# Decode attention and gated feed-forward on one core: products two pieces ahead of the sums, the last group's probabilities in a buffer of their own, and w_up in two loads

## The chip, the cores and the metric

The kernel runs on one core of a Trainium2 chip. The metric is the device time of one execution in microseconds (us); the time before is the median of three runs. Beside it stands one execution taken with the hardware profiler, whose span runs from its first to its last instruction.

## The reference

One token passes through an attention block with a cached K and V and then through a gated feed-forward block. All inputs are bf16.

```python
# x: [1,1,640]; K and V caches: [1,32,4096,128]; wq: [640,4096]; wo: [4096,640]
# w_gate, w_up: [640,1728]; w_down: [1728,640]
q = (layernorm(x) @ wq)                      # 32 heads of 128
p = softmax(q . K / sqrt(128))               # per head, over 4096 positions
h = x + (p . V) @ wo
h2 = h + (gelu(layernorm(h) @ w_gate) * (layernorm(h) @ w_up)) @ w_down
```

K and V of each head are read once: 32 heads x 4096 x 128 x 2 bytes is 33.6 MB for each cache.

## The kernel before

The 32 heads are worked in four groups of eight. A group's K is one load of 8.39 MB into a tile of 64 KB in each of the 128 partitions: a head takes 16 partitions, and each partition holds 256 positions of 128 values. V has the same layout. Three such tiles, `big[0]` to `big[2]`, are used in turn (`kb`, `vb`, lines 135 and 136). `wo_sb` and `wg_sb` lie in `big[2]`, after K of group 3 has been read, and `wu_sb` and `wd_sb` in `big[0]`, after V of group 2 has been read. In `big[2]`, w_o and w_gate take 58,240 of the 65,536 bytes of a partition.

The scores of a group are made in eight pieces of 32 positions per partition (`scores`, line 349). For a piece, VectorE multiplies K by the query in place (`mult`, line 323). TensorE then adds the 128 products of each position down to 16, by eight products with a unit matrix that accumulate in one PSUM bank (`fold`, line 329; its first product has line 336 and the other seven have line 285, that of the helper `again`). VectorE sums these 16 (`red`, line 341). Two PSUM banks, `pf[0]` and `pf[1]`, take turns, so a fold waits for the sum two pieces back (line 339). Each engine works its own list in the order in which the program writes it, and the order on VectorE is: product 0, product 1, sum 0, product 2, sum 1, and so on. After the fold of the second piece, `between` puts other work in: the second half of the queries, or the group before's `outs`.

`soft(g)` (line 362) takes the maximum of each head, the exponentials on ScalarE, and writes the probabilities into `P` spread over eight columns by a mask (line 374). `P` is one buffer for all groups, so this write waits for the value products of the group before (`t_pv[g - 1]`). `values(g)` (line 379) puts the sums of the exponentials into `rsm`, has TensorE add these over the partitions (line 382), and makes 64 products of P with V (line 386). `outs(g)` (line 392) divides, picks each head's own part and collects it in `aT`.

The order of the parts is written out by hand. From group 2 on it is:

```python
    scores(2, lambda: outs(1), ahead=True)   # ahead: the first product of group 3 as well
    load_v(3, kfree[2])
    soft(2)
    scores(3)
    values(2)
    soft(3)
    outs(2)
    values(3)
    t_aT = outs(3)
```

All large loads are issued from SyncE, in program order, on one queue. A load that reuses a tile waits on SyncE for the last reader: K and V loads for `kfree` (a group's last fold) or `vfree` (a group's last value product). The loads at the end are w_o and w_gate (`kfree[3]`), w_up (`vfree[2]`), and w_down in five pieces (`wd_sb`, line 440 and 445).

At the end of the program, the attention output is multiplied by w_o (line 472), normed, and multiplied by w_gate and then by w_up in `up` (line 483): five blocks of the 640 inputs, four products for each, with two short ones for the last 64 columns, for each matrix. The products with w_down follow (line 525), then the cast and the store.

Of the kernel before, what the change touches and what calls it, by code (L numbers as in the profile page):

```python
# [6 lines left out]
BF16 = mybir.dt.bfloat16  # L7
ALU = mybir.AluOpType
# [3 lines left out]
D = 640  # L12
# [3 lines left out]
DF = 1728  # L16
NC_D = D // 128
# [5 lines left out]
HG = 8  # L23
NG = H // HG
PPH = 128 // HG
R = SK // PPH
RP = 32
NP = R // RP
VR = 32 // HG
NV = R // VR  # L30
HB = 4
QD = 128 // HB
# [75 lines left out]
def bass_sequential_preLN__gqa_block_cached__glu_gated_geglu__decode_kernel(  # L108
# [12 lines left out]
    S = Sched(nc)  # L121

    def sb(name, shape, dt):
        return nc.alloc_sbuf_tensor(name, shape, dt)

    def at(name, base, off, shape, dt=BF16):
        return nc.alloc_sbuf_tensor_at(name, shape, dt, offset=nc.lookup_mloc(base).addr + off)

    big = [sb("big%d" % i, [128, R, DH], BF16) for i in range(3)]
    wq_sb = at("wq_sb", big[2], 0, [128, NC_D, H * DH])  # L130
    wo_sb = at("wo_sb", big[2], 0, [128, QD, D])
    wg_sb = at("wg_sb", big[2], 2 * QD * D, [128, NC_D, DF])
    wu_sb = at("wu_sb", big[0], 0, [128, NC_D, DF])
    wd_sb = at("wd_sb", big[0], 2 * NC_D * DF, [128, NF, D])
    kb = [big[0], big[2], big[1], big[2]]
    vb = [big[1], big[0], big[0], big[1]]
# [4 lines left out]
    qb = sb("qb", [128, NG, DH], BF16)  # L141
    sc = sb("sc", [128, R], FP32)
    ex = sb("ex", [128, R], BF16)
    P = sb("P", [128, R, HG], BF16)
    rs = sb("rs", [128, NG], FP32)
    rsm = sb("rsm", [128, HG], FP32)
    mx = sb("mx", [128, NG], FP32)
# [10 lines left out]
    hmask = sb("hmask", [128, HG], FP32)  # L158
# [26 lines left out]
    ones = sb("ones", [128, 128], FP32)  # L185
# [9 lines left out]
    pv, pg, pu = pq[0:2], pq[2], pq[3]  # L195
    pz = pm
    pd = pf[0]

    def vec(fn, waits=()):
        return S.op("vector", fn, waits)  # L200
# [20 lines left out]
    a = pick(jred, quad)  # L221
# [3 lines left out]
    t_hbf = vec(lambda v: v.tensor_copy(hmask_bf[:, :], hmask[:, :]), [t_hmask])  # L225

    kfree, vfree = [None] * NG, [None] * NG
# [39 lines left out]
    a = None  # L267
    for c in range(NC_D):
        a = S.op("tensor", lambda t, c=c: t.matmul(
            po[:, c:c + 1], x_sb[0:1, c::NC_D], ones_bf[0:1, 0:1],  # L270
            start=(c == 0), stop=(c == NC_D - 1), skip_group_check=True),
            [d_x, t_onebf], token=(c == NC_D - 1))
# [44 lines left out]
                t_qb[gg] = S.op("scalar", lambda a, gg=gg: a.copy(qb[:, gg, :], xz[:, :]), [t_qf[0]])  # L317

    fold_done, red_done = {}, {}
    t_p, t_pv, t_acc, t_rz, t_z = ([None] * NG for _ in range(5))  # L320
    t_ext, t_ex = None, None

    def mult(g, s):
        return vec(lambda v: v.tensor_tensor(  # L324
            out=kb[g][:, s * RP:(s + 1) * RP, :], in0=kb[g][:, s * RP:(s + 1) * RP, :],
            in1=qb[:, g, :].unsqueeze(1).to_broadcast([128, RP, DH]), op=ALU.mult),
            [d_k[g], t_qb[g]])

    def fold(g, s, t_mult):
        n = g * NP + s  # L330
        W = 512 // RP
        for j in range(DH // W):
            def mm(t, j=j):
                dst, src = pf[n % 2][:, :], kb[g][:, s * RP:(s + 1) * RP, j * W:(j + 1) * W]
                if j == 0:
                    return t.matmul(dst, Ibf[:, :], src, start=True, stop=False)  # L336
                return again(t, dst, Ibf[:, :], src, j == DH // W - 1)
            fold_done[n] = S.op("tensor", mm,
                [t_mult, t_ibf, red_done.get(n - 2)], token=(j == DH // W - 1))
# [7 lines left out]
    early = {}  # L347

    def scores(g, between=None, ahead=False):
        t_mul = early.pop(g, None) or mult(g, 0)  # L350
        for s in range(NP):
            fold(g, s, t_mul)
            if s + 1 < NP:
                t_mul = mult(g, s + 1)
            elif ahead:
                early[g + 1] = mult(g + 1, 0)
            if between and s == 1:
                between()
            red(g, s)
        kfree[g] = fold_done[g * NP + NP - 1]  # L360

    def soft(g):
        nonlocal t_ex
        a = vec(lambda v: v.reduce_max(mx[:, g:g + 1], sc[:, :], axis=AX.X), [red_done[g * NP + NP - 1]])
        a = vec(lambda v: v.transpose(mt[:, :], mx[:, g:g + 1].to_broadcast([128, 32])), [a])
        a = vec(lambda v: v.reduce_max(
            mh[:, :], mt[:, :].rearrange("p (t i) -> p t i", t=2), axis=AX.X), [a])
        a = vec(lambda v: v.scalar_tensor_tensor(  # L368
            out=mj[:, :], in0=mh[:, :], scalar=-SCALE, in1=tmask[:, :], op0=ALU.mult, op1=ALU.mult,
            accum_out=nb[:, g:g + 1]), [a, t_tmask])  # L370
        t_ex = S.op("scalar", lambda a: a.activation(  # L371
            ex[:, :], sc[:, :], ACTF.Exp, bias=nb[:, g:g + 1], scale=SCALE,
            accum_out=rs[:, g:g + 1]), [a, t_p[g - 1] if g else None])
        t_p[g] = vec(lambda v: v.tensor_tensor(  # L374
            out=P[:, :, :], in0=ex[:, :].unsqueeze(2).to_broadcast([128, R, HG]),
            in1=hmask_bf[:, :].unsqueeze(1).to_broadcast([128, R, HG]), op=ALU.mult),
            [t_ex, t_hbf, t_pv[g - 1] if g else None])

    def values(g):
        a = vec(lambda v: v.tensor_scalar(  # L380
            rsm[:, :], hmask[:, :], rs[:, g:g + 1], 0.0, ALU.mult, ALU.add), [t_ex, t_z[g - 1] if g else None])
        t_z[g] = S.op("tensor", lambda t: t.matmul(  # L382
            pz[:, 8:8 + HG], ones[:, :], rsm[:, :], start=True, stop=True), [a, t_rz[g - 1] if g else None])
        for i in range(NV):
            r, q = i * VR, 32 * (i % 4)
            t_pv[g] = S.op("tensor", lambda t, i=i, r=r, q=q: t.matmul(  # L386
                pv[g % 2][q:q + 32, :], P[:, r:r + VR, :], vb[g][:, r:r + VR, :],
                start=(i < 4), stop=(i >= NV - 4)),
                [t_p[g], d_v[g], t_qt[0], t_ext], token=(i == NV - 1))
        vfree[g] = t_pv[g]  # L390
# [39 lines left out]
    d_wo = S.dma("sync", "wo", lambda s: s.dma_start(  # L430
        wo_sb[:, :, :], A_wo[:, :].rearrange("(p c) n -> p c n", c=QD)), [kfree[3]])

    def load_w(name, dst, src, wait):
        return S.dma("sync", name, lambda s: s.dma_start(
            dst[:, :, :], src[:, :].rearrange("(p c) n -> p c n", c=NC_D)), [wait])

    d_wg = load_w("wg", wg_sb, B_w_gate, kfree[3])
    d_wu = load_w("wu", wu_sb, B_w_up, vfree[2])
    t_zr = S.op("gpsimd", lambda g: g.memset(wd_sb[:, NM, :], 0.0), [vfree[2]])
    d_we = S.dma("sync", "wde", lambda s: s.dma_start(  # L440
        wd_sb[E0:E0 + EP, NM, :], B_w_down[MF:DF, :]), [t_zr])
# [1 line left out]
    for i in range(len(WD_CUTS) - 1):  # L443
        lo, hi = WD_CUTS[i], WD_CUTS[i + 1]
# [6 lines left out]
    def clear(ps, t):  # L451
# [3 lines left out]
    t_clear = [clear(pg, t_qt[0]), clear(pu, t_qt[0])]  # L455

    a = vec(lambda v: v.tensor_tensor(
        out=aL[:, :, :], in0=aT[:, :].unsqueeze(2).to_broadcast([128, H, HB]),
        in1=jmask[:, :].unsqueeze(1).to_broadcast([128, H, HB]), op=ALU.mult), [t_aT, t_jm])
    a = S.op("tensor", lambda t: t.matmul(  # L460
        pz[:, 64:64 + QD], aL[:, :, :], csel[:, :], start=True, stop=True), [a, t_cs])
    t_aP = vec(lambda v: v.tensor_copy(aP[:, :], pz[:, 64:64 + QD]), [a])

    for j in range(4):
        S.op("tensor", lambda t, j=j: t.matmul(
            pd[32 * j:32 * j + 1, 0:NQ], ones_bf[0:1, 0:1], x_sb[0:1, j * NQ:(j + 1) * NQ],
            start=True, stop=False, skip_group_check=True), [red_done[NG * NP - 2]], token=False)
    b = None
    for c in range(QD):
        for j in range(4):  # L470
            last = c == QD - 1 and j == 3
            b = S.op("tensor", lambda t, c=c, j=j: t.matmul(
                pd[32 * j:32 * j + 1, 0:NQ], aP[:, c:c + 1], wo_sb[:, c, j * NQ:(j + 1) * NQ],
                start=False, stop=False, skip_group_check=True), [t_aP, d_wo], token=last)
    a = vec(lambda v: v.transpose(
        th[:, :].rearrange("p (c i) -> p c i", c=NC_D),
        pd[:, 0:NQ].rearrange("p (i c) -> p c i", c=NC_D)), [b])
    t_h = vec(lambda v: v.scalar_tensor_tensor(
        out=h32[:, :], in0=th[:, 0:NQ:32], scalar=1.0, in1=zero[:, :], op0=ALU.mult, op1=ALU.add,
        accum_out=st[:, 2:3]), [a])  # L480
    t_hln = layernorm(h32, t_h, 2, (hln[:, :], h32[:, :]), pz)

    def up(ps, w, d_w, t_clear):
        b = None
        for c in range(NC_D):
            for j in range(4):
                row = ps[32 * j:32 * j + 1, 0:32 * NF].rearrange("p (i b) -> p i b", b=NF)
                lhs = hln[:, c:c + 1]
                last = c == NC_D - 1 and j == 3
                b = S.op("tensor", lambda t, c=c, j=j, row=row, lhs=lhs: t.matmul(  # L490
                    row[:, :, 0:NM], lhs,
                    w[:, c, QF * j:QF * (j + 1)].rearrange("p (i b) -> p i b", b=NM),
                    start=(c == 0), stop=(c == NC_D - 1), skip_group_check=True),
                    [t_hln, d_w, t_clear], token=last)
                if E0 <= 32 * j < E0 + EP:
                    f0 = MF + 32 * j - E0
                    S.op("tensor", lambda t, c=c, j=j, f0=f0, row=row, lhs=lhs: again(
                        t, row[:, :, NM:NF], lhs, w[:, c, f0:f0 + 32].unsqueeze(2),
                        c == NC_D - 1, 32 * j), token=False)
        return b  # L500
# [9 lines left out]
    a = vec(lambda v: v.tensor_mul(t1[:, :], g_t, g_t), [t_g])  # L510
    a = vec(lambda v: v.tensor_mul(t2[:, :], t1[:, :], g_t), [a])
# [4 lines left out]
    a = vec(lambda v: v.reciprocal(r_t[:, :], d_t[:, :]), [a])  # L516
# [47 lines left out]
```

## Time and profile before

| | |
|---|---|
| median of three runs | 205.74 us (204.15, 205.74, 206.18) |
| the profiled execution's own time | 202.97 us |
| its span | 201.7 us |
| mean granted TensorE clock | 0.852 |
| busy: VectorE, TensorE products | 129.9 us (64%), 117.6 us (58%) |
| read from HBM | 84.23 MB, 418 GB/s over the span |

A row of the timeline has the start, the duration, the engine, the line and the operation with its tiles. In brackets stands how long the engine was idle just before it and what ended that. PE is TensorE, PEld its weight load, DVE is VectorE, ACT is ScalarE, SPq is the queue of SyncE. In the part on transfers the last figure is the time from the issue to the landing. A row for a stretch (two times with a colon) has the busy time of each engine, then the granted clock, the share of the transfer engines and GB/s.

### The profile page before, as it was taken

To read this page: it belongs to the slowest core of one execution; us is meant where nothing else is said; L and a number is where in the kernel's file an instruction comes from. 1 tells how busy PE (TensorE), PEld (TensorE's weight loads), DVE (VectorE), ACT (ScalarE), POOL (GpSimd) and SP (SyncE) were. 2 spreads that over 40 slices of the span, in tenths; PEclk is the share of its full clock that TensorE was granted. 3 is DMA by queue.
4 is the path that set the end of the run, shared out by engine and by line. 5 is a ranking of instruction groups with operands and counts; after the bars stand their busy time and mean duration, and the time that the engine had idled before them with its cause. 6 is when DMAs were issued, how large, how long until landed. Compare 5 with 4: busy or idle time off the path is not lost.

```text
span 201.7 us, 1610 instructions
## 1 busy us (share of the span) xinstructions
PE 117.6 (58%) x826; PEld 22.0 (11%) x552; DVE 129.9 (64%) x162; ACT 6.0 (3%) x18; POOL 1.1 (1%) x6
## 2 busy tenths in 40 slices
PE   1008383591686199497627464776197777194554
PEld 1001000000000041100003100000000003143312
DVE  5100530889898737899962598999889973804231
ACT  3000000001000100000010000000100001000000
POOL 0000000000000000000000000000000000100000
PEclk9999969679589958859985999999958999969855
DMA  7999999999999999999999999999999999999992
GB/s 260 406 556 429 429 416 416 416 416 416 416 416 482 494 455 406 429 429 416 429 416 416 419 455 507 429 429 429 416 429 416 429 416 448 393 420 417 425 401 82
DMA packets 2400, 84.32 MB, mean 418 GB/s; under 512 B 281, under 2 KB 474, under 8 KB 858
## 3 DMA queue, kind: packets, MB, share of 16 engines
q1 hardware_dynamic: 2392, 84.23, 97.1%
q8 instruction: 5, 0.08, 0.2%
q10 hardware_dynamic: 2, 0.00, 0.0%
q14 instruction: 1, 0.01, 0.0%
HBM read 84.23 MB, written 0.00 MB: 418 GB/s over the span
## 4 chain that ended last, share of the span: by engine, by line
DMA 46%; DVE 36%; PE 15%; issue 1%; ACT 1%; SPq 0%; DVEq 0%
DMA big<-in_A_k_cache_dram 34%; DVE big L324 23%; DMA wu_sb<-in_B_w_up_dram 11%; PE pf L285 6%; DVE sc L343 6%; PE pq L386 5%; DVE P L374 2%; PE pf L336 1%; DVE xm L309 1%; PE pq L490 1%; PE pf L525 1%; DVE xz L314 1%; ACT ex L371 1%; DVE xz L398 1%; PE pm L382 0%
## 5 line engine op out<-in xcount | busy, mean ns | idle before, releaser
L324 DVE TENSOR_TENSOR big<-big,qb 128x4096 bf16<-128x4096 bf16 x32 | 72.8, 2282 | 17.8 <-DMA big<-in_A_k_cache_dram 17.8
L285 PE MATMUL pf<-big,Ibf 128*128 128x512 bf16 x224 | 63.0, 428 | 0.0
L336 PE MATMUL pf<-big,Ibf 128*128 128x512 bf16 x32 | 14.3, 446 | 34.2 <-DVE big L324 34.2
L343 DVE TENSOR_REDUCE sc<-pf 128x32 f32<-128x512 f32 x32 | 21.9, 686 | 9.1 <-PE pf L285 9.0
L386 PE MATMUL pq<-big,P 128*32 128x512 bf16 x256 | 20.6, 494 | 0.0
L309 DVE TENSOR_TENSOR xm<-pq,hmask 64x512 f32<-64x512 f32 x8 | 5.5, 688 | 16.1 <-PE pq L285 15.9
L299 PE MATMUL pq<-wq_sb,xb 128*128 128x512 bf16 x10 | 4.8, 475 | 15.6 <-DMA wq_sb<-in_A_wq_dram 11.6
L336 PEld LDWEIGHTS pf<-big,Ibf 128*128 128x128 bf16 x32 | 3.5, 111 | 94.5 <-DVE big L324 94.1
L374 DVE TENSOR_TENSOR P<-ex,hmask_bf 128x2048 bf16<-128x2048 bf16 x4 | 9.2, 2292 | 5.1 <-PE pq L386 3.1
L285 PE MATMUL pq<-wq_sb,xb 128*128 128x512 bf16 x30 | 10.7, 476 | 0.0
L386 PEld LDWEIGHTS pq<-big,P 128*32 128x32 bf16 x256 | 7.8, 121 | 10.9 <-issue 7.8
L382 PE MATMUL pm<-rsm,ones 128*128 128x8 f32 x8 | 2.2, 345 | 11.3 <-DVE rsm L380 11.3
L401 PE MATMUL po<-hsel,xz 128*128 128x8 f32 x8 | 1.8, 293 | 11.7 <-DVE xz L398 11.7
L395 DVE TENSOR_TENSOR xm<-pq,rmask 128x512 f32<-128x512 f32 x4 | 2.6, 652 | 4.8 <-PE pq L386 4.8
L371 ACT ACTIVATE ex<-sc,nb 128x256 bf16<-128x256 f32 x4 | 2.0, 507 | 117.2 <-DVE mj L368 117.2
L314 DVE TENSOR_REDUCE xz<-xm 128x128 f32<-128x512 f32 x4 | 4.1, 1022 | 0.1
L398 DVE TENSOR_REDUCE xz<-xm 128x128 f32<-128x512 f32 x4 | 4.1, 1018 | 0.1
L299 PEld LDWEIGHTS pq<-wq_sb,xb 128*128 128x128 bf16 x10 | 1.2, 120 | 25.6 <-issue 20.4
L382 PEld LDWEIGHTS pm<-rsm,ones 128*128 128x128 f32 x8 | 1.8, 280 | 16.8 <-DVE rsm L380 16.8
L490 PE MATMUL pq<-wu_sb,hln 128*1 128x416 bf16 x20 | 2.2, 566 | 1.9 <-DMA wu_sb<-in_B_w_up_dram 1.9
L401 PEld LDWEIGHTS po<-hsel,xz 128*128 128x128 f32 x8 | 1.4, 218 | 16.5 <-DVE xz L398 16.5
L490 PE MATMUL pq<-wg_sb,hln 128*1 128x416 bf16 x20 | 2.2, 562 | 1.2 <-DVE hln L264 1.2
(76 smaller groups left out, 37.6 us busy)
## 6 DMA issues: line engine op xcount, KB each, us to landing
wq_sb<-in_A_wq_dram SPq DMA_DIRECT2D x1, 5120.0 KB, 15.1
wo_sb<-in_A_wo_dram SPq DMA_DIRECT2D x1, 5120.0 KB, 17.4
wg_sb<-in_B_w_gate_dram SPq DMA_DIRECT2D x1, 2160.0 KB, 22.2
wu_sb<-in_B_w_up_dram SPq DMA_DIRECT2D x1, 2160.0 KB, 22.8
wd_sb<-in_B_w_down_dram SPq DMA_DIRECT2D x1, 800.0 KB, 23.5
wd_sb<-in_B_w_down_dram SPq DMA_DIRECT2D x1, 640.0 KB, 23.7
wd_sb<-in_B_w_down_dram SPq DMA_DIRECT2D x1, 480.0 KB, 24.4
wd_sb<-in_B_w_down_dram SPq DMA_DIRECT2D x1, 160.0 KB, 24.3
```

What stands on the lines that cost most here:

```text
L285: return t.add_instruction(m)
L299: return t.matmul(dst, xb[:, c, :], src, start=(c == 0), stop=last)
L309: a = t_qt[0] = vec(lambda v, i=i, lo=lo, hi=hi, h0=h0: v.tensor_tensor(out=xm[lo:hi, :, :], in0=pq[i][lo:hi, :].rearrange("p (h d) -> p h ...
L314: t_qf[0] = vec(lambda v: v.reduce_sum(xz[:, :], xm[:, :, :].rearrange("p h d -> p d h"), axis=AX.X), [a, t_qb[gg - 1] if gg else None])
L324: return vec(lambda v: v.tensor_tensor(out=kb[g][:, s * RP:(s + 1) * RP, :], in0=kb[g][:, s * RP:(s + 1) * RP, :], in1=qb[:, g, :].unsquee ...
L336: return t.matmul(dst, Ibf[:, :], src, start=True, stop=False)
L343: red_done[n] = vec(lambda v: v.reduce_sum(sc[:, s * RP:(s + 1) * RP], pf[n % 2][:, :].rearrange("p (r w) -> p r w", r=RP), axis=AX.X), [f ...
L371: t_ex = S.op("scalar", lambda a: a.activation(ex[:, :], sc[:, :], ACTF.Exp, bias=nb[:, g:g + 1], scale=SCALE, accum_out=rs[:, g:g + 1]), ...
L374: t_p[g] = vec(lambda v: v.tensor_tensor(out=P[:, :, :], in0=ex[:, :].unsqueeze(2).to_broadcast([128, R, HG]), in1=hmask_bf[:, :].unsqueez ...
L386: t_pv[g] = S.op("tensor", lambda t, i=i, r=r, q=q: t.matmul(pv[g % 2][q:q + 32, :], P[:, r:r + VR, :], vb[g][:, r:r + VR, :], start=(i < ...
L398: t_ext = vec(lambda v: v.reduce_sum(xz[:, :], xm[:, :, :].rearrange("p r d -> p d r"), axis=AX.X), [a, t_acc[g - 1] if g else t_qb[NG - 1]])
L490: b = S.op("tensor", lambda t, c=c, j=j, row=row, lhs=lhs: t.matmul(row[:, :, 0:NM], lhs, w[:, c, QF * j:QF * (j + 1)].rearrange("p (i b) ...
```

## The change

Three things change. First, `scores` keeps two products ahead of the sums instead of one (`LOOK = 2`): VectorE's order becomes product 0, 1, 2, sum 0, product 3, sum 1, and so on, with the last three sums of a group in a row. With `ahead`, the first two products of group 3 stand among the last sums of group 2. Second, the probabilities of group 3 go to `Pl`, a buffer of 4 KB in each partition behind w_gate in `big[2]`; their write waits for the last fold of group 3 (`kfree[3]`), no longer for the value products of group 2. `rsm` is now written in `soft`, right behind the probabilities, and no longer in `values`. Third, w_up is loaded in two parts, three fifths and two fifths of its blocks, and each block's products wait for their own part. The lines below `LOOK` move down by one to three.

```diff
+LOOK = 2
...
-    P = sb("P", [128, R, HG], BF16)
+    P = [sb("P", [128, R, HG], BF16)] * (NG - 1) + [at("Pl", big[2], 2 * (QD * D + NC_D * DF), [128, R, HG])]
...
     def scores(g, between=None, ahead=False):
-        t_mul = early.pop(g, None) or mult(g, 0)
+        t_mul = early.pop(g, None) or {s: mult(g, s) for s in range(LOOK)}
+        nxt = early.setdefault(g + 1, {}) if ahead else {}
         for s in range(NP):
-            fold(g, s, t_mul)
-            if s + 1 < NP:
-                t_mul = mult(g, s + 1)
+            fold(g, s, t_mul[s])
+            if s + LOOK < NP:
+                t_mul[s + LOOK] = mult(g, s + LOOK)
             elif ahead:
-                early[g + 1] = mult(g + 1, 0)
+                nxt[s + LOOK - NP] = mult(g + 1, s + LOOK - NP)
             if between and s == 1:
                 between()
             red(g, s)
...
         t_p[g] = vec(lambda v: v.tensor_tensor(
-            out=P[:, :, :], in0=ex[:, :].unsqueeze(2).to_broadcast([128, R, HG]),
+            out=P[g][:, :, :], in0=ex[:, :].unsqueeze(2).to_broadcast([128, R, HG]),
             in1=hmask_bf[:, :].unsqueeze(1).to_broadcast([128, R, HG]), op=ALU.mult),
-            [t_ex, t_hbf, t_pv[g - 1] if g else None])
+            [t_ex, t_hbf, kfree[g] if g == NG - 1 else t_pv[g - 1] if g else None])
+        t_rs[g] = vec(lambda v: v.tensor_scalar(
+            rsm[:, :], hmask[:, :], rs[:, g:g + 1], 0.0, ALU.mult, ALU.add), [t_ex, t_z[g - 1] if g else None])
 
     def values(g):
-        a = vec(lambda v: v.tensor_scalar(
-            rsm[:, :], hmask[:, :], rs[:, g:g + 1], 0.0, ALU.mult, ALU.add), [t_ex, t_z[g - 1] if g else None])
         t_z[g] = S.op("tensor", lambda t: t.matmul(
-            pz[:, 8:8 + HG], ones[:, :], rsm[:, :], start=True, stop=True), [a, t_rz[g - 1] if g else None])
+            pz[:, 8:8 + HG], ones[:, :], rsm[:, :], start=True, stop=True), [t_rs[g], t_rz[g - 1] if g else None])
...
-    def load_w(name, dst, src, wait):
-        return S.dma("sync", name, lambda s: s.dma_start(
-            dst[:, :, :], src[:, :].rearrange("(p c) n -> p c n", c=NC_D)), [wait])
-
-    d_wg = load_w("wg", wg_sb, B_w_gate, kfree[3])
-    d_wu = load_w("wu", wu_sb, B_w_up, vfree[2])
+    def load_w(name, dst, src, lo, hi, wait):
+        return [S.dma("sync", name, lambda s: s.dma_start(
+            dst[:, lo:hi, :], src[:, :].rearrange("(p c) n -> p c n", c=NC_D)[:, lo:hi, :]), [wait])] * (hi - lo)
+
+    d_wg = load_w("wg", wg_sb, B_w_gate, 0, NC_D, kfree[3])
+    d_wu = load_w("wu", wu_sb, B_w_up, 0, 3, vfree[2])
+    d_wu += load_w("wv", wu_sb, B_w_up, 3, NC_D, vfree[2])
...
-                    [t_hln, d_w, t_clear], token=last)
+                    [t_hln, d_w[c], t_clear], token=last)
```

More of the change, by code (lines that the diff above doesn't have):

```diff
@@ L319, in bass_sequential_preLN__gqa_block_cached__glu_gated_geglu__decode_kernel @@
     fold_done, red_done = {}, {}
-    t_p, t_pv, t_acc, t_rz, t_z = ([None] * NG for _ in range(5))
+    t_p, t_pv, t_acc, t_rz, t_rs, t_z = ([None] * NG for _ in range(6))
     t_ext, t_ex = None, None
@@ L386, in values @@
             t_pv[g] = S.op("tensor", lambda t, i=i, r=r, q=q: t.matmul(
-                pv[g % 2][q:q + 32, :], P[:, r:r + VR, :], vb[g][:, r:r + VR, :],
+                pv[g % 2][q:q + 32, :], P[g][:, r:r + VR, :], vb[g][:, r:r + VR, :],
                 start=(i < 4), stop=(i >= NV - 4)),
```

## The prediction

> **What bounds the kernel now.** First the page: the DMA row in slices, the bytes, and the chain that ended last.
>
> ```profile
> DMA  7999999999999999999999999999999999999992
> HBM read 84.23 MB, written 0.00 MB: 418 GB/s over the span
> DMA 46%; DVE 36%; PE 15%; issue 1%; ACT 1%; SPq 0%; DVEq 0%
> ```
>
> The chain gives VectorE 36%, which invites work on VectorE. The first row corrects that: the transfers are busy in every slice but the first and the last, also where the chain runs over VectorE. The chain in order of time shows their pace.
>
> ```profile
> 1.25 33.99 DMA big<-in_A_k_cache_dram
> ...
> 78.07 35.22 DMA big<-in_A_k_cache_dram
> ```
>
> K of group 0 lands at 1.25 + 33.99 = 35.24, K of group 2 at 113.29. Between them land V0, K1, V1 and K2, four loads of 8.39 MB (128 x 64 KB): 78.05 / 4 = 19.5 us each, 430 GB/s. K3, V2 and V3 follow, so V3 lands near 113.29 + 3 x 19.5 = 171.8. 84.23 MB at 430 GB/s are 196 us of a span of 201.7: the transfer stream has some 3 us of room besides its start and the output.
>
> Next, what is issued last, when it lands (page, last part), and the timeline of the end.
>
> ```profile
> wq_sb<-in_A_wq_dram SPq DMA_DIRECT2D x1, 5120.0 KB, 15.1
> wo_sb<-in_A_wo_dram SPq DMA_DIRECT2D x1, 5120.0 KB, 17.4
> wg_sb<-in_B_w_gate_dram SPq DMA_DIRECT2D x1, 2160.0 KB, 22.2
> wu_sb<-in_B_w_up_dram SPq DMA_DIRECT2D x1, 2160.0 KB, 22.8
> wd_sb<-in_B_w_down_dram SPq DMA_DIRECT2D x1, 800.0 KB, 23.5
> wd_sb<-in_B_w_down_dram SPq DMA_DIRECT2D x1, 640.0 KB, 23.7
> wd_sb<-in_B_w_down_dram SPq DMA_DIRECT2D x1, 480.0 KB, 24.4
> wd_sb<-in_B_w_down_dram SPq DMA_DIRECT2D x1, 160.0 KB, 24.3
> wd_sb<-in_B_w_down_dram SPq DMA_DIRECT2D x1, 80.0 KB, 22.3
> ```
>
> ```profile
> 166.43 0.33 SPq L430 DMA_DIRECT2D wo_sb<-in_A_wo_dram  x1
> 166.80 0.43 SPq L434 DMA_DIRECT2D wg_sb<-in_B_w_gate_dram  x1
> ...
> 194.16 0.91 PE L490 MATMUL pq<-wu_sb,hln 128*1 128x416 bf16 x5 [1.92 <-DMA wu_sb<-in_B_w_up_dram]
> ...
> 197.51 2.15 PE L525 MATMUL pf<-wd_sb,hm 128*1 128x160 bf16 x56 [1.04 <-DVE hm L519]
> 198.95 0.23 PEld L525 LDWEIGHTS pf<-wd_sb,hm 128*1 128x1 bf16 x12 [0.28 <-DMA wd_sb<-in_B_w_down_dram]
> 199.34 0.09 PEld L525 LDWEIGHTS pf<-wd_sb,hm 128*1 128x1 bf16 x4 [0.16 <-DMA wd_sb<-in_B_w_down_dram]
> ```
>
> w_o lands at 166.43 + 17.4 = 183.8, w_gate at 166.80 + 22.2 = 189.0, w_up at 194.1, where its wait ends. The last products wait for two pieces of w_down, at 198.95 and 199.34. So in this execution the end is the landing of the last piece of w_down plus four products, the cast and the store. The arithmetic runs ahead of the loads by little: w_up's products were held 1.92 us by their load, and the last products lost 0.28 + 0.16. Arithmetic may thus be 1.92 + 0.44 = 2.4 us later before it sets the end. The stream has a second margin: w_o must be issued before V3 is through. Its issue needs at most 2.9 us to take effect (wq: 15.1 us for 5.24 MB that take 12.2 at 430 GB/s), so 166.43 + 2.9 = 169.3 against 171.8, 2.5 us. Both margins are about 2.4 us.
>
> **The change part by part.** Its span lies around group 3, in this timeline.
>
> ```profile
> 146.71 0.61 PE L336 MATMUL pf<-big,Ibf 128*128 128x512 bf16 x1 [4.99 <-DVE big L324]
> 147.11 3.19 PE L285 MATMUL pf<-big,Ibf 128*128 128x512 bf16 x7
> 150.34 0.69 DVE L343 TENSOR_REDUCE sc<-pf 128x32 f32<-128x512 f32 x1 [0.89 <-PE pf L285]
> ...
> 164.72 1.67 PE L285 MATMUL pf<-big,Ibf 128*128 128x512 bf16 x7
> 166.43 0.69 DVE L343 TENSOR_REDUCE sc<-pf 128x32 f32<-128x512 f32 x1 [1.40 <-PE pf L285]
> ...
> 167.64 3.64 PE L386 MATMUL pq<-big,P 128*32 128x512 bf16 x64
> ...
> 168.70 0.19 ACT L371 ACTIVATION_READ_ACCUMULATOR ex<-sc,nb 128x1 f32 x1
> ...
> 171.40 2.29 DVE L374 TENSOR_TENSOR P<-ex,hmask_bf 128x2048 bf16<-128x2048 bf16 x1 [3.14 <-PE pq L386]
> ...
> 176.78 5.05 PE L386 MATMUL pq<-big,P 128*32 128x512 bf16 x64
> ...
> 185.13 2.38 PE L472 MATMUL pf<-wo_sb,aP 128*1 128x160 bf16 x128
> 189.94 0.91 PE L490 MATMUL pq<-wg_sb,hln 128*1 128x416 bf16 x5 [1.18 <-DVE hln L264]
> ```
>
> *Products two ahead.* The same 32 products and 32 sums are issued, in another order; nothing is added. A fold still needs the sum two pieces back, since there are two PSUM banks (line 339). Before, the eighth product of a group follows sum 5; after, it precedes it, but its fold must wait for sum 5. Either way the last fold of a group starts after 8 products and 6 sums. At full clock the edit gives nothing. What it does take away are sums that wait for a slow fold in mid-group: here 0.89 us at 150.34. All such waits are in one row:
>
> ```profile
> DVE sc L343 <- PE pf L285: 9.0, 8, 1.5
> ```
>
> Four of the eight are the group ends, as the 1.40 at 166.43, and stay. Those of groups 0 and 1 can only bring forward the issue of K and V loads, and the DMA row shows the queue never empty there. On group 3 I take 0.9 (bounds 0 and 0.9): last fold and w_o's issue at 165.5 instead of 166.4. The price of its cover: products held in front of the first sum delay nothing, as no transfer waits for a sum.
>
> *rsm moved into the softmax, probabilities of group 3 in Pl.* One operation changes place, none is added. Before, group 2's value products began at 167.64, behind the last sum and rsm, 1.25 after the last fold; after, they need only their own small sum product: 165.5 + 0.4 = 165.9, done at 169.6. So w_up is issued 1.7 us earlier, behind w_gate in the queue either way: nothing. P of group 3 waited on VectorE, idle for 3.14 us, until those products were done at 171.3; behind it stood rz, xm, xz and aT of group 2. In its own buffer it needs the exponentials (168.9) and the last fold of K3, long done: 168.9 - 0.9 - 0.1 for rsm = 167.9, 3.5 earlier. All behind it moves alike, so group 3's value products start near 176.8 - 3.5 = 173.3; V3 (171.8) is in by then, though not by much: with V3 late, this gain stops there. The attention result is ready at 181.6 instead of 185.1, and now w_o is late next: its products start at 183.9, a gain of 1.2. The gate's products move from 189.94 to 189.0, where w_gate's landing holds them: 0.9.
>
> *w_up in two loads.* Same bytes, one issue and one set of landings more. The first three fifths land near 189.0 + 0.6 x 5.1 = 192.1; 12 of 20 products (and their short companions) run before the rest lands at 194.1. All 20 took from 194.16 to 197.51 - 1.04 = 196.47, 2.3 us; the 8 that remain take 0.4 x 2.3 = 0.9. hm is ready 1.4 us earlier. Its last products then wait for w_down at 198.95 and 199.34 as before. Cost of a further load: w_down is 2160 KB in five loads, 194.1 to 199.34, 5.2 us; w_up is 2160 KB in one, 189.0 to 194.1, 5.1 us. That is 0.03 us for each; from below, 0, since the bytes are the same.
>
> *Sum.* Stream 0 to -0.9 if the earlier w_o issue is of use (it sits behind V3, so I take 0), +0.03 for the load, arithmetic -1.4 at hm, all of it swallowed by w_down's landing. Against the profiled execution's own time: 202.97 + 0.0 = 203.0 us.
>
> **How that stands to the runs.** The three runs gave 204.15, 205.74 and 206.18, 1.2 to 3.2 us above this execution. A program whose end is a stream of fixed bytes should not spread by that; something that differs from run to run must reach the end. One such thing shows within this one execution: the clock.
>
> ```profile
> 146.70:150.30 3.60, 3.59 (x9) 0.25 (x2) 2.75 (x2) 0.00 (x0) 0.00 (x0) 0.50 1.14 492
> 107.50:113.10 5.60, 5.57 (x65) 2.06 (x65) 0.00 (x0) 0.00 (x0) 0.00 (x0) 0.65 0.92 398
> 167.60:171.30 3.70, 3.67 (x65) 1.62 (x65) 0.57 (x4) 0.60 (x2) 0.00 (x0) 1.00 0.86 370
> ```
>
> The granted clock is the third figure from the end, before the DMA share and GB/s. At 0.50 seven folds take 3.19 us, at full clock 1.67; 64 value products take 5.57 at 0.65 and 3.64 at 1.00. Had group 3's last fold and group 2's values fallen into half clock, 1.5 + 1.9 us, and one more sum been held 0.9, the arithmetic would be 4.3 us late, and 4.3 - 2.4 = 1.9 would reach the end: 204.9, inside the spread of the runs. After the change the same lateness meets a margin of 2.4 + 3.5 in the arithmetic, and w_o's issue is late by 1.5 - 0.9 only, under 2.5. It would vanish. The Trainium skill, "TensorE: Matmul & The Clock Gate", section on the HAM clock gate, says that the activity window which decides the clock is free-running, so that the slow stretch falls differently from run to run; the half clock after 4.99 us of idle at 146.71 agrees, the variation from run to run no trace here shows.
>
> **Forecast and rivals.**
> *Forecast: the runs lose their arithmetic lateness.* They come down to the stream, 203.0, with 0.3 (a tenth of the median's excess of 2.8, my choice) for lateness above the new margin: 203.3 us, 1.2% under the median. Chance 0.50.
>
> *Rival 1: the lateness of the runs is the transfers' own.* Slower packets or a later first transfer in some executions would spread the end just so, and nothing here removes that. For it: the end of the profiled execution is a landing, and 430 GB/s leaves no room to catch up. Then 205.74 - 0.2 = 205.5. Chance 0.34.
>
> *Rival 2: the two banks undo the products ahead, and V3 stops the rest.* Only the 1.4 at hm and part of the values' gain are of use in late runs: half the excess of 2.8 goes, 204.3. The change would do less than its words. Chance 0.07.
>
> *Rival 3, slower: a further load costs a serial start.* It decides if the second part of w_up does not begin while the first is under way; the price is the start-up of wq, 2.9 us, everything behind it (w_down) moves by that: 205.74 + 2.5 = 208.2. Against it: five pieces of w_down cost 0.1 together. Chance 0.09. The Trainium skill, "DMA: Bandwidth & Descriptors", "Anatomy of one DMA", gives a fixed cost of about 2.0 us to each DMA; serial, it would be an estimate of 207.7. The landings of w_down speak against its being serial in a full queue.
>
> **How the numbers follow.** 1% of 205.74 is 2.1 us, about what a measurement of this kernel tells from no change. Faster by more: the forecast's 0.50. Within: rivals 1 and 2, 0.41. Slower: 0.09. The range: low end 202.1, the stream with w_o's earlier issue fully of use (203.0 - 0.9); high end 206.3, rival 1 with the upper of the runs (206.18) and the added load; rival 3 is left out. The forecast's own range is 202.5 to 204.1.
>
> **What would show it.** Right: the wait of L374 for the products of L386 in group 3 is gone and Pl is written by 170; group 3's value products start at 172 to 174; w_o's products wait for their DMA; 8 of w_up's products remain after its second landing; the last LDWEIGHTS of w_down still wait for a DMA near 199.3, and the profiled span is within 0.7 us of 201.7. Wrong: a profiled span under 200.5 (the stream had gaps that I do not see), the last landing over 200.5 (the second load costs a start), or runs that spread as widely as before about the same median (rival 1).

## The result, and the profile after

| | before | after |
|---|---|---|
| median of eleven runs, same chip | 204.53 us (203.56 to 206.18) | 202.91 us (202.86 to 203.51) |
| runs at or below 203.3 us | 0 of 11 | 10 of 11 |
| the profiled execution's own time | 202.97 us | 202.86 us |
| its span | 201.7 us | 201.6 us |

The change is 0.83% faster: the ratio is 0.9917, 95% interval 0.9888 to 0.9946. (Ratios leave out executions more than 1.5% above a kernel's fastest.) That is real, and inside the predicted range, but below the 1% that the forecast had called faster. Eleven runs put the kernel before at 204.53; the three that the prediction worked from had given 205.74.

The two profiled executions hardly differ in time. The gain is in the other executions: after the change they sit within 0.7 us of the fastest, before it they spread over 2.6 us.

First the page of after: its DMA row in slices, the bytes, and the time from issue to landing of the last loads.

```profile
DMA  7999999999999999999999999999999999999992
HBM read 84.23 MB, written 0.00 MB: 418 GB/s over the span
wo_sb<-in_A_wo_dram SPq DMA_DIRECT2D x1, 5120.0 KB, 17.6
wu_sb<-in_B_w_up_dram SPq DMA_DIRECT2D x1, 1296.0 KB, 22.1
wu_sb<-in_B_w_up_dram SPq DMA_DIRECT2D x1, 864.0 KB, 23.9
```

The transfers are as before, to the GB/s. Now the timeline of after, on the same stretches as before; the rows between these are left out.

```profile
150.56 2.79 PE L286 MATMUL pf<-big,Ibf 128*128 128x512 bf16 x7
152.15 0.69 DVE L344 TENSOR_REDUCE sc<-pf 128x32 f32<-128x512 f32 x1
166.10 0.33 SPq L432 DMA_DIRECT2D wo_sb<-in_A_wo_dram  x1
166.12 3.64 PE L388 MATMUL pq<-big,P 128*32 128x512 bf16 x64
168.59 2.29 DVE L376 TENSOR_TENSOR Pl<-ex,hmask_bf 128x2048 bf16<-128x2048 bf16 x1 [0.67 <-ACT ex L373]
173.34 5.28 PE L388 MATMUL pq<-big,Pl 128*32 128x512 bf16 x64
183.84 3.86 PE L475 MATMUL pf<-wo_sb,aP 128*1 128x160 bf16 x128 [2.04 <-DMA wo_sb<-in_A_wo_dram]
190.13 0.72 PE L493 MATMUL pq<-wg_sb,hln 128*1 128x416 bf16 x5 [1.18 <-DVE hln L265]
194.08 0.54 PE L493 MATMUL pq<-wu_sb,hln 128*1 128x416 bf16 x5 [0.55 <-DMA wu_sb<-in_B_w_up_dram]
194.27 0.38 PE L493 MATMUL pq<-wu_sb,hln 128*1 128x416 bf16 x3
195.73 0.24 PE L528 MATMUL pf<-wd_sb,hm 128*1 128x160 bf16 x4 [1.04 <-DVE hm L522]
198.84 0.70 PE L528 MATMUL pf<-wd_sb,hm 128*1 128x160 bf16 x16 [0.46 <-DMA wd_sb<-in_B_w_down_dram]
```

Three things are to be seen. A slow fold (150.56, 2.79 us instead of 1.67) no longer holds the sum at 152.15: that row has no bracket. Pl is written behind the exponentials, not behind the value products of group 2. And w_o's, w_up's and w_down's products all wait for a DMA: the arithmetic runs ahead of the loads to the end. But w_o's 128 products took 3.86 us, where they took 2.38 before.

The view of waits gives the sums' waits of after in one row (total us, number, longest), against 9.0, 8, 1.5 before, and what TensorE waited for its loads at the end:

```profile
DVE sc L344 <- PE pf L286: 4.9, 4, 1.5
...
PE pf L475 <- DMA wo_sb<-in_A_wo_dram: 2.0, 1, 2.0
...
PE pf L528 <- DMA wd_sb<-in_B_w_down_dram: 1.6, 3, 0.9
...
PE pq L493 <- DMA wu_sb<-in_B_w_up_dram: 0.5, 1, 0.5
```

The four waits that stay are the group ends, as foretold. By these waits, the arithmetic of this execution could have been 2.0 + 1.6 + 0.5 = 4.1 us later, had its clock stayed the same.

### The profile page after: what moved, and what is told of

It reads as the page before. It is cut to its first block, busy times and chain, and to the rows that moved or that the text cites. A ratio compares the mean times of both kernels' runs of the same rounds, so it can differ in the third digit from the quotient of the medians.

```text
span 201.6 us, 1632 instructions
## 1 busy us (share of the span) xinstructions
PE 117.3 (58%) x826; PEld 22.9 (11%) x552; DVE 129.8 (64%) x162; ACT 6.0 (3%) x18; POOL 1.1 (1%) x6
## 4 chain that ended last, share of the span: by engine, by line
DMA 49%; DVE 38%; PE 9%; SPq 1%; issue 1%; ACT 1%
DMA big<-in_A_k_cache_dram 36%; DVE big L325 25%; DMA wd_sb<-in_B_w_down_dram 13%; DVE sc L344 6%; PE pq L388 5%; PE pf L286 3%; DVE P L376 2%; DVE xm L310 1%; DVE xz L315 1%; ACT ex L373 1%; DVE xz L400 1%; SPq L448 0%; SPq L436 0%; PE pf L337 0%; DVE mx L366 0%
## 5 line engine op out<-in xcount | busy, mean ns | idle before, releaser
L388 PE MATMUL pq<-big,P 128*32 128x512 bf16 x192 | 15.7, 499 | 0.0
L376 DVE TENSOR_TENSOR P<-ex,hmask_bf 128x2048 bf16<-128x2048 bf16 x3 | 6.9, 2292 | 2.0 <-ACT ex L373 2.0
L388 PEld LDWEIGHTS pq<-big,P 128*32 128x32 bf16 x192 | 6.0, 122 | 8.3 <-issue 6.1
L388 PE MATMUL pq<-big,Pl 128*32 128x512 bf16 x64 | 5.3, 502 | 0.0
L475 PE MATMUL pf<-wo_sb,aP 128*1 128x160 bf16 x128 | 3.9, 309 | 2.0 <-DMA wo_sb<-in_A_wo_dram 2.0
L475 PEld LDWEIGHTS pf<-wo_sb,aP 128*1 128x1 bf16 x128 | 3.7, 114 | 2.2 <-issue 2.2
```

The costliest lines, as they stand in the source:

```text
L376: t_p[g] = vec(lambda v: v.tensor_tensor(out=P[g][:, :, :], in0=ex[:, :].unsqueeze(2).to_broadcast([128, R, HG]), in1=hmask_bf[:, :].unsqu ...
L388: t_pv[g] = S.op("tensor", lambda t, i=i, r=r, q=q: t.matmul(pv[g % 2][q:q + 32, :], P[g][:, r:r + VR, :], vb[g][:, r:r + VR, :], start=(i ...
L475: b = S.op("tensor", lambda t, c=c, j=j: t.matmul(pd[32 * j:32 * j + 1, 0:NQ], aP[:, c:c + 1], wo_sb[:, c, j * NQ:(j + 1) * NQ], start=Fal ...
```

## The experiments

The theory: an execution ends at the later of two things, the transfer stream (202.7 to 203.0 us in the best runs of all kernels but two: 203.20 with the two loads alone, 206.50 with twelve operations of delay) and the arithmetic, and the runs above that are arithmetic made late by half clock. The rival: the lateness is the transfers' own. Each kernel was run beside the kernel before. On the three chips used its medians were 204.24 (for the first four rows), 204.08 (after without the two loads, fillers in front and tail, the two rows of delay alone) and 204.36 (the rest), with 4 of 35, 7 of 29 and 4 of 32 runs at or below 203.3.

| kernel | median, us | at or below 203.3 | ratio to before, 95% |
|---|---|---|---|
| before, once more | 204.06 | 3 of 12 | 0.9987 (0.9956 to 1.0019) |
| products two ahead alone | 202.99 | 8 of 12 | 0.9976 (0.9945 to 1.0006) |
| Pl and rsm alone | 203.69 | 3 of 12 | 0.9984 (0.9954 to 1.0014) |
| w_up in two loads alone | 204.51 | 2 of 12 | 1.0004 (0.9963 to 1.0045) |
| after without the two loads | 203.18 | 7 of 12 | 0.9959 (0.9931 to 0.9987) |
| before, fillers in front and tail | 203.13 | 9 of 12 | 0.9975 (0.9945 to 1.0004) |
| before, fillers in front | 202.97 | 7 of 9 | 0.9940 (0.9917 to 0.9964) |
| before, fillers in the tail | 204.40 | 2 of 12 | 1.0006 (0.9975 to 1.0037) |
| after, 6 operations of delay | 204.59 | 2 of 12 | 1.0014 (0.9975 to 1.0053) |
| after, 12 operations of delay | 207.51 | 0 of 6 | 1.0157 (1.0106 to 1.0208) |
| after, 6 of delay and fillers | 202.94 | 9 of 12 | 0.9962 (0.9939 to 0.9985) |
| after, fillers | 203.09 | 9 of 12 | 0.9952 (0.9930 to 0.9974) |

**The kernel before, once more.** No edit; what was wanted is a profile of one of its late executions.

> The kernel before itself, for a second profile and for the spread of its times. Late arithmetic: its runs spread from 203.5 to 206, and where a profile falls into a late one, group 3 has more half clock than in the first profile and hm of the end is late, while the transfers keep 19.5 us per K or V load. Late transfers: in a late run the loads of K and V take longer than 19.5 us each or start later, and the products wait for them.

Its profiled execution took 206.24 us. The last stretch of its chain in order of time, and the timeline from w_o's issue to w_o's products:

```profile
188.31 4.46 PE pf L472 x96
...
200.88 2.06 PE pf L525 x50
```

```profile
168.20 0.33 SPq L430 DMA_DIRECT2D wo_sb<-in_A_wo_dram  x1
178.76 6.21 PE L386 MATMUL pq<-big,P 128*32 128x512 bf16 x64
188.31 4.44 PE L472 MATMUL pf<-wo_sb,aP 128*1 128x160 bf16 x128
```

In this late execution no load stands in the chain from w_o's products on: arithmetic sets the end. w_o was issued at 168.20 (166.43 in the first profile), the values of group 3 took 6.21 us (5.05) and w_o's products 4.44 (2.38).

**Products two ahead alone.**

```diff
+LOOK = 2        # one P, rsm in values, w_up in one load, as before
```

> Only the products two ahead; one P, rsm in values, w_up in one load. Late arithmetic: it takes a held sum (0.9 us) off the excess of about 1.6 us over the stream, 203.7 to 204.0. If the late issue of w_o is what costs, this part alone moves it (0.3 to 0.9 us earlier) and gives all of the gain, 203.0. Two banks undo it: 204.4.

202.99 us. The twelve runs form two clusters, eight at 202.8 to 203.2 and four at 204.2 to 204.8; the interval reaches 1, the counts (8 of 12 against 4 of 35) speak for an effect. Its profile fell in the upper cluster:

```profile
166.73 0.33 SPq L432 DMA_DIRECT2D wo_sb<-in_A_wo_dram  x1
177.29 5.83 PE L388 MATMUL pq<-big,P 128*32 128x512 bf16 x64
186.48 4.43 PE L474 MATMUL pf<-wo_sb,aP 128*1 128x160 bf16 x128
...
199.05 2.04 PE L527 MATMUL pf<-wd_sb,hm 128*1 128x160 bf16 x56 [1.06 <-DVE hm L521]
```

The front is on time (166.73); what is left above the floor is the tail at half clock, and w_down's products wait for hm, not for a DMA.

**Pl and rsm alone.**

```diff
 LOOK = 1        # w_up in one load
+P = [...] * (NG - 1) + [Pl];  rsm written in soft
```

> Only the own buffer for group 3 and rsm in the softmax; products one ahead, w_up in one load. Late arithmetic: the values of group 3 start 2.6 us or more earlier, more than the excess of most runs, so 203.1. If the late issue of w_o is what costs: 204.5, as kfree is not moved. If only the stretch from w_up's landing to hm costs: 204.5.

203.69 us, between before and after; but the interval holds 1, and 3 of 12 against 4 of 35 is no clear difference, so an effect of this part alone is not shown. In its profile the tail starts early, as in after (values of group 3 at 174.51, 176.78 in the first profile of before), but the front is late: w_o is issued at 167.27, 166.43 in the first profile.

**w_up in two loads alone.**

```diff
 LOOK = 1        # one P, rsm in values
+d_wu = load_w("wu", wu_sb, B_w_up, 0, 3, vfree[2])
+d_wu += load_w("wv", wu_sb, B_w_up, 3, NC_D, vfree[2])
```

> Only w_up in two loads. Late arithmetic: hm follows the gate's products more closely, up to 1.4 us, but only where w_up's landing and not the gate's products hold it, 203.7 to 204.4. If the stretch from w_up's landing to hm is what costs: 203.0. A serial start of a further load: 206 or more.

204.51 us, no effect. Its profiled execution (204.76 us) shows a late front in the old order; VectorE's timeline behind the landing of K2, then the rest:

```profile
113.46 4.49 DVE L325 TENSOR_TENSOR big<-big,qb 128x4096 bf16<-128x4096 bf16 x2 [8.51 <-DMA big<-in_A_k_cache_dram]
...
119.00 0.69 DVE L344 TENSOR_REDUCE sc<-pf 128x32 f32<-128x512 f32 x1 [1.05 <-PE pf L286]
...
127.73 0.69 DVE L344 TENSOR_REDUCE sc<-pf 128x32 f32<-128x512 f32 x1 [0.46 <-PE pf L286]
```

```profile
168.58 0.33 SPq L432 DMA_DIRECT2D wo_sb<-in_A_wo_dram  x1
179.07 6.33 PE L388 MATMUL pq<-big,P 128*32 128x512 bf16 x64
188.72 3.65 PE L475 MATMUL pf<-wo_sb,aP 128*1 128x160 bf16 x128
...
200.31 1.14 PE L528 MATMUL pf<-wd_sb,hm 128*1 128x160 bf16 x56 [1.50 <-DVE hm L522]
```

Behind K2's landing VectorE makes two products and then stands 1.05 us for the first fold, whose seven products take 2.93 us instead of 1.67. The same stretch in windows, this kernel's row first, then that of after:

```profile
113.00:121.00 8.00, 5.19 (x16) 0.24 (x2) 6.49 (x4) 0.00 (x0) 0.00 (x0) 0.79 0.93 401
```

```profile
113.00:121.00 8.00, 4.99 (x20) 0.20 (x2) 7.44 (x5) 0.00 (x0) 0.00 (x0) 0.79 1.00 434
```

At the same granted clock, 0.79, VectorE is busy 6.49 us in the one and 7.44 in the other: 0.95 us apart. That is the held sum, 1.05, less the 0.10 us by which K2 lands later in after. The timeline of after has three products in a row there and the sum without a bracket:

```profile
113.56 6.70 DVE L325 TENSOR_TENSOR big<-big,qb 128x4096 bf16<-128x4096 bf16 x3 [7.13 <-DMA big<-in_A_k_cache_dram]
120.18 0.68 DVE L344 TENSOR_REDUCE sc<-pf 128x32 f32<-128x512 f32 x1
```

From K2's landing to w_o's issue the late execution takes 168.58 - 113.46 = 55.1 us and after 166.10 - 113.56 = 52.5. The profile of before used for the prediction had 1.00 in this window and took 166.43 - 113.31 = 53.1, with one sum held in mid-group (0.89 us): it had been one of the fortunate ones.

**After without the two loads.**

```diff
-d_wu = load_w("wu", wu_sb, B_w_up, 0, 3, vfree[2])
-d_wu += load_w("wv", wu_sb, B_w_up, 3, NC_D, vfree[2])
+d_wu = load_w("wu", wu_sb, B_w_up, 0, NC_D, vfree[2])
```

> The kernel after with w_up in one load again. If all of the gain lies ahead of w_up's landing: 202.9, spread as after. If w_up's landing to hm still reaches the end when its load is late by 0.5 us, as in the profile of the buffer alone: median 203.0 to 203.4 and more spread.

203.18 us, 7 of 12 at or below 203.3, against 202.91 and 10 of 11. The two loads show no effect on the kernel before, and perhaps 0.3 us on one whose arithmetic is already near the loads; the intervals overlap, so that is not shown.

**The clock by itself.** Fillers are products of the identity with itself into an unused part of PSUM, queued on TensorE where it would idle. They change no order and no wait of the other instructions; they are there to keep the clock up. First at all four places:

```diff
 values(1)
+busy(45)             # busy(n): n products Ibf x Ibf into pq[3][:, 0:128]
 ...
+            if g == 3 and s == 0:
+                busy(70)     # behind the first fold of group 3
 ...
 values(2)
+busy(60)
 ...
 values(3)
+busy(25)
```

> The kernel before with 200 products of the unit matrix with itself added on TensorE, into PSUM columns that nobody reads, in four places where TensorE sits idle (after the values of group 1, after the first fold of group 3, after the values of groups 2 and 3). Order, waits and loads are those of before. Half clock after idle time as the cause of the late arithmetic: the folds, values and w_o products behind those places run at full clock, and the runs come down from 204.2 to 203.0, spread under 0.7. Late transfers: 204.2 as before. Added work in the way: 205 or more.

203.13 us with nothing of the change in it. Then the front (45, 70) and the tail (60, 25) apart:

> The kernel before with only the first two groups of added products (45 after the values of group 1, 70 after the first fold of group 3). If the sums held behind half-clock folds carry the lateness: 203.0 to 203.4, as the products two ahead alone. If the tail (values of group 3 and w_o's products at half clock) carries it: 203.8 to 204.1.

> The kernel before with only the last two groups of added products (60 after the values of group 2, 25 after those of group 3). If the tail carries the lateness (values of group 3 6.2 instead of 3.6 us, w_o's products 4.5 instead of 2.4): up to 4 us less in late runs, 203.1 with the rest the transfers' own spread. If the held sums carry it: 203.8 to 204.1.

Front: 202.97 us, the whole gain within its uncertainty. Tail: 204.40, nothing. The timeline of the front kernel, behind K2's landing and around the 70 fillers, and that of the tail kernel at its end:

```profile
116.46 2.99 PE L285 MATMUL pf<-big,Ibf 128*128 128x512 bf16 x7
...
119.49 0.69 DVE L343 TENSOR_REDUCE sc<-pf 128x32 f32<-128x512 f32 x1 [1.11 <-PE pf L285]
...
143.39 4.02 PE L285 MATMUL pq<-Ibf 128*128 128x128 bf16 x69
148.48 0.39 PE L336 MATMUL pf<-big,Ibf 128*128 128x512 bf16 x1 [1.08 <-DVE big L324]
148.71 1.67 PE L285 MATMUL pf<-big,Ibf 128*128 128x512 bf16 x7
```

```profile
167.63 0.33 SPq L440 DMA_DIRECT2D wo_sb<-in_A_wo_dram  x1
177.77 3.64 PE L388 MATMUL pq<-big,P 128*32 128x512 bf16 x64
185.30 4.00 PE L482 MATMUL pf<-wo_sb,aP 128*1 128x160 bf16 x128 [0.70 <-DMA wo_sb<-in_A_wo_dram]
...
195.48 0.91 PE L500 MATMUL pq<-wu_sb,hln 128*1 128x416 bf16 x5 [1.76 <-DMA wu_sb<-in_B_w_up_dram]
...
200.73 0.09 PEld L535 LDWEIGHTS pf<-wd_sb,hm 128*1 128x1 bf16 x4 [0.17 <-DMA wd_sb<-in_B_w_down_dram]
```

In the front kernel group 3's second fold takes 1.67 us instead of 3.19, and no sum of group 3 is held in mid-group. Group 2's first fold is not helped: the 45 fillers end 2.22 us before it, it takes 2.99 us, and its sum is held 1.11 us (2.97 and 1.26 in the profile of the kernel with all four places). So what the two profiles show taken away is the 0.89 us of group 3. The median fell by more, 1.4 us; what the 45 fillers did in the other executions is not shown.

In the tail kernel's profile (205.20 us) the values of group 3 run at full clock (3.64), and it is late all the same, because the loads are: w_o's products wait for their load at 185.30, w_up's until 195.48 (194.16 in the first profile), and the last wait for w_down ends at 200.73 (199.34). Some 0.8 us of its time is not explained by this: the time lies 2.1 us above the span, where the others lie 1.2 to 1.3 above theirs. So the front's lateness does something that the tail's clock cannot make good.

**How much the tail of after can bear.** Operations on VectorE ahead of the softmax of group 3, six and twelve, planned at 0.65 us each (3.9 and 7.8 us); six again with 110 and 25 fillers behind the values of groups 2 and 3; and after with 50 and 25 fillers alone.

```diff
 values(2)
+for _ in range(6):   # or 12; a product of two constants into xm, not used
+    t_qf[0] = vec(...tensor_tensor(out=xm, in0=ones, in1=rmask, op=ALU.mult), [t_qf[0], t_ext])
 soft(3)
```

> The kernel after with six VectorE operations of 0.65 us (128x512, written to a scratch tile) put ahead of the softmax of group 3: the arithmetic behind the last sum is 3.9 us later, loads and issues are not touched. In the profile after, w_o's products wait 2.0 us for their load and the end has 1.7 us and a few tenths more: margin 4.0. Late arithmetic against the stream: 203.0 to 203.6 with more spread. If the margin is nil: 206.8.

> The same with twelve such operations, 7.8 us later. Late arithmetic against a margin of 4.0: 202.9 + 3.8 = 206.7. If the issue of w_o is what decides: 202.9, since it does not move.

> The kernel after with the six late operations (3.9 us) and 110 + 25 added products behind the values of groups 2 and 3. If half clock in the tail is what made the margin of the kernel after small (it read 204.6 with the six alone): the values and w_o's products at full clock give 3 us back, 203.0. If the margin is small for another reason: 204.6.

> The kernel after with 50 + 25 added products in the same two places, for a version that stays on the transfer stream: 202.9, no faster than the kernel after in the median, as the last landing sets the end; the runs above 203.2 fewer, as far as they are arithmetic and not transfers.

The group of the six operations in the kernel's lines (busy us, mean ns of one, idle us before):

```profile
L428 DVE TENSOR_TENSOR xm<-ones,rmask 128x512 f32<-128x512 f32 x6 | 4.1, 690 | 0.2
```

So the six took 4.1 us, not 3.9, and the twelve, at the same 0.69 us each, 8.3. Six cost 204.59 - 202.91 = 1.7 us, twelve 207.51 - 202.91 = 4.6: by the medians the margin is 4.1 - 1.7 = 2.4 and 8.3 - 4.6 = 3.7 us. With fillers the same six cost nothing (202.94). So what reaches the end of the delay goes with half clock in the tail; with the clock kept up, after bears 4.1 us. Fillers alone add nothing to after (203.09): at its median the arithmetic is not what ends it. The timelines of the last two kernels, the one with delay first:

```profile
177.88 3.64 PE L390 MATMUL pq<-big,Pl 128*32 128x512 bf16 x64
184.82 2.38 PE L489 MATMUL pf<-wo_sb,aP 128*1 128x160 bf16 x128
```

```profile
174.26 3.64 PE L390 MATMUL pq<-big,Pl 128*32 128x512 bf16 x64
185.35 4.15 PE L485 MATMUL pf<-wo_sb,aP 128*1 128x160 bf16 x128 [4.26 <-DMA wo_sb<-in_A_wo_dram]
```

Starting the values 3.6 us sooner, the second has TensorE idle 4.26 us for w_o's load, which is late here (185.35), and w_o's products then take 4.15 us instead of 2.38. In all four profiles in which these products wait for their load they take 3.86 to 4.44 us. Of the ten in which they do not, six have them at 2.38 us and four at 3.64 to 4.44. So waiting for a load goes with a low clock here, but it is not the only way to it, and no run changed the wait alone.

## Why the prediction held, and where it did not

*Right: the end.* A landing of w_down plus the last products, the cast and the store set the profiled end: 202.86 us against 203.0 by the sum.

*Right: where the steps would land.* Pl is written from 168.59 to 170.88 (by 170 was said: 0.9 late), group 3's value products start at 173.34 (173.3), w_o's products at 183.84 and wait for their load (183.9), eight of w_up's products follow its second landing, and the last wait for w_down ends at 198.84 (near 199.3). hm, by the start of the products that need it, came 1.8 us sooner (1.4).

*Right in the cause, only in part in the way: the runs' excess.* Fillers in front act on the clock alone and bring the kernel before from 204.36 to 202.97 (ratio 0.9940, interval 0.9917 to 0.9964), so the clock makes the excess. How it reaches the end differs. In three late profiles, before once more (206.24 us), the two loads alone (204.76) and products two ahead alone (204.40), no product from w_o on waits for a load: late arithmetic, as predicted. In six others above 203.3 us (203.54 to 205.20; only the kernel with twelve operations of delay is left aside) the last products wait for w_down, until 199.82 to 200.73 (199.34 in the first profile): there the loads are late. Rival 1 said slower packets, or a later first transfer. V3's load in the tail kernel's profile, its issue and its time to landing:

```profile
140.38 0.33 SPq L238 DMA_DIRECT2D big<-in_A_v_cache_dram  x1
...
big<-in_A_v_cache_dram SPq DMA_DIRECT2D x1, 31.4
```

That is 171.8, as before, and all fourteen profiles have 171.4 to 171.9. So K and V are never late, and neither is the first transfer. The lateness of the loads begins behind V3, with w_o; slower packets there are not ruled out.

*Mis-sized: products two ahead.* "On group 3 I take 0.9 (bounds 0 and 0.9)", read from a profile in which group 2 began at full clock. In a late execution (the two loads alone) the old order holds sums by 1.05 and 0.46 us behind group 2's first folds too; with the 0.89 of group 3 that is 2.4 us. From K2's landing to w_o's issue the new order is 2.6 us shorter than that execution, and 0.6 shorter than the fortunate profile. By the medians, the part that the sum gave the least carries most of the gain: alone it gave 202.99, the buffer 203.69, the two loads 204.51. The intervals of the three overlap, so this order is likely and not shown.

*Wrong: the places of half clock.* The prediction laid the lateness into group 3's last fold (1.5) and group 2's values (1.9). The values of group 2 took 3.64 us in every profile, and group 3's last fold was at full clock (1.67) as well. Half clock was found behind idle time: in group 2's first folds (not in the first profile), in group 3's second fold (the third with products two ahead), in the values of group 3 (5.05 to 6.33 where no filler stands ahead of them) and in w_o's products (2.38 to 4.44).

*Wrong: "The gate's products move from 189.94 to 189.0."* They started at 190.13. w_o's products began 1.3 us sooner, waited 2.04 us for their load, and then ran at a lower clock: 3.86 us instead of 2.38, 1.5 more. In windows, before first, then after, the granted clock is the third figure from the end:

```profile
184.00:190.00 6.00, 3.25 (x140) 2.71 (x141) 1.89 (x12) 0.46 (x2) 0.00 (x0) 0.99 1.00 426
```

```profile
184.00:190.00 6.00, 4.08 (x130) 3.78 (x122) 1.14 (x7) 0.46 (x2) 0.00 (x0) 0.76 1.00 423
```

It cost nothing, since w_up and w_down land no sooner.

*Mis-sized: the margin after, 2.4 + 3.5 = 5.9 us.* The runs gave 2.4 to 3.7; the waits of the one good execution show 4.1, a gain of 1.7 over the 2.4 of before. The step that failed is to add the 3.5 whole: 1.3 of it reached the start of w_o's products, which then gave 1.5 back.

*Wrong: the price of "faster".* The mechanism was right and the size 0.8%, not 1.2%, because 205.74 was the median of three runs, two of them among the highest that the kernel gave. The forecast, 203.3, was 0.4 above the result; its allowance of 0.3 for lateness above the new margin was not needed at the median.

*Rivals 2 and 3.* Two PSUM banks do not undo the products ahead: these take away the waits of sums in mid-group, and the last fold's place in the order stays. Rival 3's sum does not follow from its own price: 205.74 + 2.9 would be 208.6, not 208.2. The second load costs nothing that can be seen: the two parts of w_up land at about 191.9 and 194.1, and 2.2 us for 0.88 MB is what 430 GB/s gives (2.1). The Trainium skill, "DMA: Bandwidth & Descriptors", section "Anatomy of one DMA — SWDGE (gpsimd) path", has about 2.0 us fixed for each DMA, fitted to those that GpSimd issues; these loads are issued from SyncE, and between the two landings there is no room for such a time in series.

*Open.* Whether a late issue of w_o itself delays the loads behind V3. Executions with w_o issued at 165.9 to 166.8 had it landed by about 183.7 to 184.0, those at 167.2 to 167.3 at 184.0 to 184.6, those from 167.6 on at 184.3 to 185.1. That fits the tail kernel. But two profiles do not keep to the order (issued at 166.54, landed at 184.6; at 167.02, landed at 185.2), and no run moved the issue alone. The prediction's margin for it, 2.5 us after 166.43, is probably too large; that was not shown.

## What to carry to other kernels

A single profile is one draw of the clock. This kernel ends in a stream of fixed bytes, and yet its runs spread by more than 1%: a second chain lay just under the stream. In such a case look for what varies from one profile to the next (here the fold behind an idle stretch), and add up how far it may slip before it sets the end. An engine that another must keep in step with is best given work ahead, so that a slow burst of its neighbour doesn't hold it. And don't count an earlier start as margin in full: here w_o's products, started 1.3 us sooner, gave 1.5 us back in clock.

## What the runs showed of the hardware

In the first profile of before, its second, and that of the two loads alone, the programs do the same up to w_up's load. The 128 products of w_o took 2.38, 4.44 and 3.65 us in them, the 64 value products of group 3 5.05, 6.21 and 6.33. The Trainium skill, "TensorE: Matmul & The Clock Gate", section "The HAM clock gate", calls the count of slow products variable from run to run, which these rows show, and the ramp's cost under 1% of a typical span; here fillers in front, which act on the clock alone, were worth 0.6% (ratio 0.9940), through a VectorE queue that waits for the folds and a tail close to its loads.

Idle TensorE time can be filled to keep the clock, if the fillers reach far enough: 69 products without use in 4.02 us, ending about 1 us before it, held group 3's second fold at 1.67 us, while the 45 that ended 2.22 us before group 2's first fold left it at 2.99. In front fillers were worth about as much as the whole change. In the tail of before, or added to after, they were worth nothing that can be seen; in after with a tail delayed by 4.1 us they took 204.59 down to 202.94.
